# Storing a step's 32 output rows as one transfer of four quarters, or as four transfers of 32 partitions

## The chip, the core and the metric

The kernel runs on one core of a Trainium2 chip. The metric is device time in microseconds (us) for one execution; where several runs are given, their median counts. The core has five engines with instruction queues of their own: TensorE (PE), which multiplies matrices and loads weights for that beside it (PEld); VectorE (DVE); ScalarE (ACT); GpSimd (POOL); and SyncE (SP), which in this kernel only issues transfers. Transfers between main memory (HBM) and the core's on-chip memory of 128 partitions (SBUF) are moved by 16 DMA engines. An engine that issues a transfer goes on at once; when the bytes have landed, a semaphore is raised, and whoever needs them waits for it. Accumulators of matrix products lie in PSUM, from where ACT or DVE copy them out.

## The reference, cut to what matters

The output is two halves side by side. Part B (a long convolution of a state-space model) is finished before the part that this change touches. Part A is an attention with a recurrent memory: 64 segments of 32 tokens, one after the other, each with 8 memory rows that are the result of the segment before.

```python
for s in range(n_seg):                      # 64 segments of seg_len = 32
    xs = x[:, s * seg_len:(s + 1) * seg_len, :].copy()
    h = jnp.concatenate([mem, xs], axis=1)  # 8 memory rows + 32 tokens, Dm = 1024
    q = jnp.einsum('btd,dhe->bhte', h, Wq)  # 32 heads of 128
    k = jnp.einsum('btd,dhe->bhte', h, Wk)
    v = jnp.einsum('btd,dhe->bhte', h, Wv)
    scores = jnp.einsum('bhqe,bhke->bhqk', q, k) * scale
    scores = jnp.where(mask[None, None], scores, -1000000000.0)
    p = _softmax(scores, axis=-1)
    o = jnp.einsum('bhqk,bhke->bhqe', p, v)
    o = jnp.einsum('bhte,hed->btd', o, Wo)
    mem = o[:, :M, :].copy()                # M = 8
    outs.append(o[:, M:, :])
```

Everything is bf16. The weights Wq, Wk, Wv and Wo are 8 MB each; a segment needs all of them, and the next segment cannot start before the memory rows of this one are there.

## The kernel before, in words

Part A is `part_a` (L233). Its loop over `s` (L363) does one segment, called a step here, in about 20 us. 24 tokens' worth of every segment and the 8 memory rows go through the loop as one 32-column block `hT`; the other 8 tokens (their projections were made earlier) come in as small blocks from HBM and are finished after the loop (L592 to L623).

**Weights.** A weight block is 128 x 2048 bf16, 512 KB; a step uses 64 of them. 49 stay in SBUF, three are kept in PSUM and in odd places (`KEPT`, L29), and twelve are streamed again in every step from HBM into four slots `wst` that take turns (`SLOTS`, `stage`, L294 to L298). SP issues the twelve loads, each as soon as PE is done with the block that had the slot before. In the order of use, and by the names that the prediction gives them, they are

- L1: k, half 0, block 2; L2: q, half 0, block 2
- L3 and L4: k, half 1, blocks 1 and 5
- L5: q, half 1, block 4
- L6 and L7: v, half 0, blocks 2 and 7
- L8 and L9: v, half 1, blocks 4 and 7
- L10, L11, L12: output projection, blocks 4, 8 and 13

L1 to L4 of a step are issued during the step before.

**The order on PE** in a step (L484 to L580): the products k0, q0 and the first three blocks of k1 (`quads`, L364), the transposes of k0 and q0 (`tr`, L380), the rest of k1, the scores of the first half, q1, three blocks of v0, transposes of k1 and q1, the rest of v0, scores of the second half, v1, the products with the softmax weights, and the output projection (`oproj`, L474). Then the result is copied out into `ob`, its memory rows are transposed into `hT`, and the next step's k0 begins.

**The order on ACT**: copies of accumulators (`evac`, L375; its copy is L377), the exponentials, and four transfers in a step, which all stand in ACT's instruction queue. At the end of a step come the copies into `ob` (L574, L585, L588), `load_pk` for the next step (L333; called PK here), and `stores` (L348): first the store of the left-over block into `OLd` (L349; called OL), then the store of the 32 output rows (L353). Next on ACT's queue stand the copies of k0 and of q0 of the next step (both L377), the mask (L390), the copy of the transposed q0 (L497) and `load_vx` (L339; called VX).

**The rows in SBUF.** `ob[:, 0, :]` is 128 partitions x 256 elements: partitions 32q to 32q+31 hold the 32 rows of quarter q of the 1024 output columns (24 rows of tokens, and 8 memory rows whose places in the output are written again by L623 at the end). In HBM a row is 2048 elements wide (both parts), so each partition's 512 bytes go to a place of their own.

**What is written over `ob`.** `ob` lies in `arena`, a block whose regions are used again by hand (`AT`, L36). Its bytes are written next in the following step by the copy of q1 (`evac`, L377) and by the normalised weights (`weigh`, L423), which wait until the stores have landed.

**Completion semaphores.** The transfers of SP and ACT share eight completion semaphores (in the built program DMAHW0 to DMAHW7), handed out in turn when the program is built, over both queues together. A transfer waits, in its engine's queue, until the transfer that had its semaphore before has landed, which is the one eight places earlier in that turn. A step has 16 transfers, two whole turns: PK, OL, L5, the rows, L6, L7, VX, L8, L9, L10, L11, L12, and the next step's L1, L2, L3, L4.

Of the kernel before, what the change touches and what calls it, by code (L numbers as in the profile page):

```python
# [232 lines left out]
def part_a(ctx, tc, x, src, WD, HE, seg_len, out_a, ahead, W_res, rest, places, first):  # L233
    nc = tc.nc
# [47 lines left out]
    def at(name, *dims):  # L282

        n = int(np.prod(dims))
        t_ = arena[:, AT[name] // 2:AT[name] // 2 + n]
        if len(dims) == 1:
            return t_
        names = "abc"[:len(dims)]
        return t_.rearrange("p (%s) -> p %s" % (" ".join(names), " ".join(names)), **dict(zip(names, dims)))
# [58 lines left out]
    def stores(s, ob):  # L348
        nc.scalar.dma_start(out=OLd[s // 8][:, 256 * (s % 8):256 * (s % 8) + 256], in_=ob[:, 1, :])  # L349
        rows = out_a[s * SL:s * SL + SL, :].rearrange("r (q d) -> q r d", q=4)  # L350
        if s + 1 < NS:

            nc.scalar.dma_start(out=rows, in_=ob[:, 0, :])  # L353
        else:
            for q in range(4):
                nc.scalar.dma_start(out=rows[q][0:XM], in_=ob[32 * q:32 * q + XM, 0, :])
# [6 lines left out]
    for s in range(NS):  # L363
# [207 lines left out]
        ob = at("ob", 2, 256)  # L571
# [17 lines left out]
        if s + 1 < NS:  # L589
            stores(s, ob)  # L590
# [3 lines left out]
    for u in order:  # L594
        if ("o", u) in W_res:
            wo[u] = W_res["o", u]
        else:
# [3 lines left out]
            else:  # L601
                nc.sync.dma_start(out=wo[u][:].rearrange("e (h d) -> e h d", h=2), in_=src(("o", u)))
    stores(NS - 1, ob)
    for j in range(2, 8):
        nc.sync.dma_start(out=raw[j][:], in_=OLd[j])
# [926 lines left out]
```

## Time and profile before

| | |
|---|---|
| median of 3 runs | 2060.81 us (2054.64 to 2061.03) |
| profiled execution: its time, its span | 2054.64 us, 2054.6 us |
| PE busy in the span | 1873.8 us (91%) |
| ACT busy | 1051.7 us (51%) |
| stretch 760 to 1975 us (61 steps): PE busy, DMA share | 1162.56 of 1215 us, 0.95 |
| the same: bytes moved | 339 GB/s |
| last stage after the loop (L617) | about 55 us |

The steps run from about 720 us to 1994 us. In a profile, a line such as "L377 ACT CAST arena<-acc" is one group of instructions by source line, engine, operation and the names of what is written and read. "ACTq" and "SPq" are the instructions on ACT's and SP's queues that issue transfers. "idle before, releaser" is how long an engine sat before such instructions, and whose end let it go on.

### The profile page before, as it was taken

The page shows a single profiled execution, that of the slowest core. Times are in us where ns is not written, and L with a number is a line of the kernel's source. Part 1 is how long each engine was busy: PE and PEld are TensorE (multiplying, and loading weights), DVE is VectorE, ACT ScalarE, POOL GpSimd, SP SyncE. Part 2 cuts the span into 40 slices and gives each one's busy share as a digit, 9 for nine tenths or more (in the row PEclk, how much of TensorE's full clock was granted, in tenths as well). Part 3 has the DMA queues.
Part 4 walks back from the last instruction along what each step waited for, and adds up shares of the span by engine and source line. Part 5 has one row for each costly group of instructions (what it writes and reads, how often), then busy time and mean ns, then how long its engine had stood idle before and what let it go on. Part 6 is the DMA issues. An engine that isn't in the chain of part 4 may idle for free. (4 is left out here: it accounts for less than half of the span.)

```text
span 2054.6 us, 78607 instructions
## 1 busy us (share of the span) xinstructions
PE 1873.8 (91%) x33734; PEld 1187.8 (58%) x33734; DVE 1413.7 (69%) x3352; ACT 1051.7 (51%) x1981; POOL 398.5 (19%) x778
## 2 busy tenths in 40 slices
PE   2699999977999879999999999999999999999999
PEld 1365666666888535555555555555555555555554
DVE  8689989989999436666566666666666666656650
ACT  5899999961333324444344444444444444444430
POOL 2133343356000001111111111111111111111120
PEclk9999999989999989999999999999999999999999
DMA  7697986676646999999999999999999999999991
GB/s 192 176 247 217 262 227 181 164 207 204 217 140 190 330 328 350 349 337 335 315 347 342 343 339 342 343 342 339 347 345 333 339 332 341 335 333 339 342 356 46
DMA packets 349617, 590.25 MB, mean 287 GB/s; under 512 B 108536, under 2 KB 226520, under 8 KB 347220
## 3 DMA queue, kind: packets, MB, share of 16 engines
q1 hardware_dynamic: 294488, 526.49, 75.5%
q0 software_dynamic: 9968, 30.48, 4.5%
q10 hardware_dynamic: 44812, 28.26, 4.4%
q8 instruction: 264, 4.33, 0.9%
q14 instruction: 85, 0.70, 0.1%
HBM read 530.34 MB, written 65.26 MB: 290 GB/s over the span
## 5 line engine op out<-in xcount | busy, mean ns | idle before, releaser
L371 PEld LDWEIGHTS <-a_hT 128*32 128x32 bf16 x12352 | 334.4, 96 | 306.5 <-issue 59.4
L377 ACT CAST arena<-acc 128x512 bf16<-128x512 f32 x384 | 225.1, 586 | 375.6 <-PE acc L371 318.8
L371 PE MATMUL acc<-W,a_hT 128*32 128x512 bf16 x4608 | 371.7, 381 | 1.4 <-issue 1.2
L481 PEld LDWEIGHTS <-arena 128*32 128x32 bf16 x8256 | 212.1, 97 | 98.3 <-issue 47.1
L371 PE MATMUL acc<-wst,a_hT 128*32 128x512 bf16 x2304 | 231.9, 381 | 21.0 <-DMA wst<-WD_v 12.4
L292 DVE TENSOR_SCALAR arena<-keep 128x256 int32<-128x256 int32 (+1 forms) x512 | 176.3, 395 | 43.3 <-PE acc L371 39.8
L385 POOL COPY arena<-arena 128x128 bf16<-128x128 bf16 x128 | 37.5, 293 | 855.0 <-DMA arena<-PKd 312.3
L371 PE MATMUL acc<-MF,a_hT 128*32 128x512 bf16 x2048 | 171.3, 382 | 0.0
L481 PE MATMUL pp<-W_o,arena 128*32 128x256 bf16 x4096 | 138.4, 275 | 5.9 <-DMA W_o<-in_A_Wo_dram 5.8
L420 DVE TENSOR_REDUCE a_mx<-sc 128x4 f32<-128x160 f32 (+1 forms) x192 | 73.0, 380 | 81.8 <-ACT sc L416 81.8
L167 PE MATMUL pro<-xTl,wsl 128*128 128x512 bf16 x512 | 119.3, 384 | 9.6 <-ACT xTl L111 5.5
L412 DVE TENSOR_REDUCE a_mx<-sc 128x4 f32<-128x160 f32 (+1 forms) x192 | 72.0, 375 | 79.7 <-PE sc L400 78.2
L416 ACT ACTIVATE sc<-sc 128x160 f32<-128x160 f32 (+1 forms) x192 | 63.9, 333 | 120.9 <-DVE sc L413 101.8
L1066 PEld LDWEIGHTS <-MF 128*128 128x128 bf16 x1024 | 103.0, 101 | 29.9 <-issue 8.5
L443 POOL TENSOR_TENSOR arena<-arena,a_BD 128x128 bf16<-128x128 bf16 x128 | 71.2, 557 | 239.1 <-DVE arena L430 216.1
L496 DVE COPY arena<-tr 128x512 bf16<-128x512 bf16 x64 | 27.2, 425 | 128.3 <-PE tr L382 128.3
L1066 PE MATMUL hps<-KT,MF 128*128 128x256 bf16 x720 | 94.8, 285 | 14.0 <-DVE x L1235 11.0
L467 ACT CAST arena<-pv 128x256 bf16<-128x256 f32 (+1 forms) x192 | 79.0, 449 | 53.3 <-PE pp L450 41.0
L1293 PE MATMUL yp<-Bt,MI 128*128 128x256 bf16 x680 | 102.8, 273 | 0.8 <-ACT yb L1309 0.8
L574 ACT CAST arena<-pp 128x128 bf16<-128x128 f32 x128 | 27.7, 269 | 142.4 <-PE pp L481 142.4
L1104 ACT ACTIVATE E<-pa 128x648 bf16<-128x648 f32 x128 | 91.4, 714 | 17.6 <-PE pa L1096 12.1
L371 PE MATMUL acc<-W_v,a_hT 128*32 128x512 bf16 x1280 | 93.0, 380 | 0.5 <-issue 0.5
(314 smaller groups left out, 3988.2 us busy)
## 6 DMA issues: line engine op xcount, KB each, us to landing
wst<-WD_v SPq DMA_DIRECT2D x256, 512.0 KB
wst<-WD_k SPq DMA_DIRECT2D x192, 512.0 KB
wst<-WD_o SPq DMA_DIRECT2D x192, 512.0 KB
wst<-WD_q SPq DMA_DIRECT2D x128, 512.0 KB
Ud<-ux POOLq DMA_DIRECT2D x16, 1024.0 KB, 5.1
uq<-Ud SPq DMA_DIRECT2D x32, 512.0 KB
wsl<-in_A_Wk_dram SPq DMA_DIRECT2D x16, 512.0 KB
wsl<-in_A_Wv_dram SPq DMA_DIRECT2D x16, 512.0 KB
```

Of the source, the lines that this page charges most:

```text
L167: nc.tensor.matmul(a[:], lhsT=w[:, kc, 128 * j:128 * j + 128], rhs=xTl[:, kc, :, :].rearrange("p s k -> p (s k)"), start=(kc == 0), stop=( ...
L292: nc.vector.tensor_scalar(out=out.bitcast(I32), in0=in_.bitcast(I32), scalar1=0, scalar2=None, op0=ALU.bitwise_or)
L371: nc.tensor.matmul(a[32 * g:32 * g + 32, o_:o_ + rhs.shape[1]], lhsT=hT[:, kc, :], rhs=rhs, start=(kc == 0), stop=(kc == KC - 1), tile_pos ...
L377: nc.scalar.copy(out=q, in_=a[:])
L412: nc.vector.tensor_reduce(out=m_, in_=x, axis=AX.X, op=ALU.max)
L420: nc.vector.tensor_reduce(out=m_, in_=x, axis=AX.X, op=ALU.add)
L443: nc.gpsimd.tensor_tensor(out=L[:, 0].rearrange("p (a b) k -> p a b k", a=4), in0=bc(lt[:, :, 0:XL].unsqueeze(2), [128, 4, 4, XL]), in1=bc ...
L467: nc.scalar.copy(out=o[:, i:i + n], in_=p[:, i:i + n, :].rearrange("p a (g q) -> p a g q", g=4))
L481: nc.tensor.matmul(po[32 * qt:32 * qt + 32, o_:o_ + rhs.shape[1]], lhsT=oT[:, h % 4, (h % 16) // 4, :], rhs=rhs, start=False, stop=(h == 3 ...
L1066: pe.matmul(s_[r][half][:, cs, :], lhsT=MF[:, kc, 4 * rr + mc, cs, :], rhs=rhs, start=(i == 0 and mc == 0), stop=(i == 1 and mc == 3), ski ...
L1104: sc.activation(out=T["E", r, e // 4][:, lo:lo + 8 * NE].rearrange("p (i c) -> p i c", i=2), in_=T.pop(("p", r, e))[:, :, 0:4 * NE], func= ...
L1293: pe.matmul(yp[:, b, :], lhsT=m_[:, b, cs, kc, :], rhs=Bt[:, kc, j, half, c_, :], start=(kc == 0 and cs == 0 and half == 0), stop=(kc == 3 ...
```

## The change

In `stores`, the transfer of the output rows, for every step but the last, becomes a loop of four transfers, one for each quarter of the columns. They are issued by the same engine at the same place in its queue, and move the same bytes in the same 512-byte pieces. The last step already had such a loop over 24 of the 32 partitions of each quarter (L356), which stays.

```diff
         rows = out_a[s * SL:s * SL + SL, :].rearrange("r (q d) -> q r d", q=4)
         if s + 1 < NS:
 
-            nc.scalar.dma_start(out=rows, in_=ob[:, 0, :])
+            for q in range(4):
+                nc.scalar.dma_start(out=rows[q], in_=ob[32 * q:32 * q + 32, 0, :])
         else:
             for q in range(4):
                 nc.scalar.dma_start(out=rows[q][0:XM], in_=ob[32 * q:32 * q + XM, 0, :])
```

The order of all other instructions on every engine stays as it was. The number of transfers of SP and ACT in a step goes from 16 to 19, and the eight completion semaphores are handed out over these.

## The prediction

> **What bounds the kernel now.** I read the page first, then the stretch of the steps, then PE's waits in it. The change acts 63 times, once at each boundary between two steps, so the stretch from 760 to 1975 us (61 steps) is what counts. Columns: stretch, its length, busy time of PE, PEld, DVE, ACT and POOL, TensorE clock, DMA share, GB/s.
>
> ```profile
> 760.00:1975.00 1215.00, 1162.56 (x26046) 682.78 (x26041) 763.13 (x2391) 548.79 (x1287) 176.98 (x429) 1.00 0.95 339
> ```
>
> PE is busy 1162.56 of 1215 us at full clock, and the DMA engines carry 339 GB/s without a pause. Who made PE wait there (us in total, times, longest):
>
> ```profile
> PE acc L371 <- DMA wst<-WD_v: 9.1, 16, 1.2
> PE pp L481 <- DMA wst<-WD_o: 7.3, 13, 1.1
> PE acc L371 <- DMA wst<-WD_k: 4.8, 9, 1.5
> PE tr L382 <- ACT arena L377: 2.3, 3, 1.4
> PE acc L371 <- DMA wst<-WD_q: 1.4, 4, 0.5
> ```
>
> Weights cost PE only 22.6 us in 61 steps (0.37 us a step): PE is the bound, but the stream runs just ahead of it. From the landing events of the loads, step by step, a load lands at a median of 0.26 to 0.78 us before PE uses it. That is all the slack there is.
>
> Now one boundary, ACT and then SP in order of time:
>
> ```profile
> 1754.46 0.33 ACTq L333 DMA_DIRECT2D arena<-PKd  x1
> ...
> 1755.20 0.33 ACTq L349 DMA_DIRECT2D OLd<-arena  x1
> 1755.57 0.57 ACTq L353 DMA_DIRECT2D out_dram<-arena  x1
> 1757.29 0.59 ACT L377 CAST arena<-acc 128x512 bf16<-128x512 f32 x1 [2.12 <-PE acc L371]
> 1758.95 0.59 ACT L377 CAST arena<-acc 128x512 bf16<-128x512 f32 x1 [1.08 <-PE acc L371]
> 1759.57 0.43 ACT L390 CAST sc<-a_mask 128x320 f32<-128x320 bf16 x1
> ```
>
> ```profile
> 1752.67 2.60 SPq L297 DMA_DIRECT2D wst<-WD_k  x2
> 1755.87 0.32 SPq L297 DMA_DIRECT2D wst<-WD_q  x1
> 1757.81 5.51 SPq L297 DMA_DIRECT2D wst<-WD_v  x4
> ```
>
> ACT issues the rows at 1755.57 and has 1.15 us to spare before k0's copy. SP issues L3 and L4, then L5, then L6 at 1757.81. In the chain of work the pieces named DMA run from issue to landing:
>
> ```profile
> 1736.81 7.50 DMA out_dram<-arena
> ...
> 1755.87 6.65 DMA wst<-WD_q
> ...
> 1769.04 7.16 DMA wst<-WD_k
> ```
>
> A transfer takes 5 to 7 us, because some four loads are queued. From the landing events, with time zero at the issue of OL, medians of 39 steps: L1 lands at -0.27, L2 at 1.44, L3 at 3.24 (one in ten after 4.27), L4 at 5.13, PK at 5.18, OL at 5.58, L5 at 6.80, the rows at 6.71, L6 (issued at 2.62) at 8.30, L7 (issued at 4.13) at 10.01, L8 (issued at 5.68) at 11.57.
>
> **The change, part by part.** The sum is made against the profiled execution (2054.6 us, whose own time 2054.64 is the lowest of the three); it is then put on the median, 2060.81.
>
> *Three more issues on ACT, 63 times.* The rows of L353 and L356:
>
> ```profile
> L353 ACTq DMA_DIRECT2D out_dram<-arena x63: 552/562/1144, 741.9 to 1974.0; - x63
> L356 ACTq DMA_DIRECT2D out_dram<-arena x4: 308/444/675, 1995.4 to 1997.7; - x4
>   ACT arena L377: 6.8, 6
>   DVE arena L423: 3.3, 4
> ```
>
> One issue of 562 ns becomes four of 308 to 444 ns: 1.23 to 1.78 us, that is 0.7 to 1.2 us more. k0's copy follows 1.15 us after the old issue, so by itself this is hidden.
>
> *The turn of the eight semaphores.* This I take to be the main effect. With 19 transfers in a step the turn is PK, OL, L5, R0, R1, R2, R3, L6, L7, VX, L8 to L12, L1 to L4 (R0 to R3 are the four pieces), and each waits for the one eight places earlier. In the listing of the built kernel R0 waits for L12, R1 for L1, R2 for L2, R3 for L3; L6 for L4, L7 for PK, VX for OL, L8 for L5, and L9 to L12 for R0 to R3. Before, the rows waited for L12 and L6 for nothing later than L2.
> That ACT does stand still for such a wait shows in the last step, which has the split already:
>
> ```profile
> 1995.35 2.65 ACTq L356 DMA_DIRECT2D out_dram<-arena  x4
> ```
>
> Its four issues last 0.68, 0.51, 0.38 and 0.31 us, 1.88 together; of the 2.65, 0.70 us lie before the fourth, which goes 0.02 us after the load with its semaphore before it (an L600 load) has landed.
>
> (a) ACT. R3 cannot be issued before L3 has landed, at 3.24, and ends at 3.57. Behind it on ACT stand k0's copy (2.09 before, then 3.6 to 4.2) and q0's (3.75 before, then 4.2 to 4.8); PE's transposes of q0 (L382) wait for that, then the copy of L497 and the scores. I moved the two copies in each of the 39 steps to where that step's landing of L3 lets them: q0's copy comes 0.37 us later in the mean (median 0.22, one in ten over 0.84). PE has nothing else to do there, so 0.37 us a step is on the path.
>
> (b) SP. L6 goes at 5.18 instead of 2.62 (2.33 us late in the mean), L7 at 5.5 instead of 4.13, L8 at 6.85 instead of 5.68. When L6 is issued, only L5 and small pieces are still queued, so it should travel faster than its 5.56 us. Four 512 KB loads that met an empty queue in part B (uq, L1040) landed 3.69 to 4.01 us after issue. So L6 lands at 8.9 to 9.2. PE wants it at 8.30 + 0.37 slack + 0.37 from (a) = 9.04: between nothing and 0.16 us; L7 and L8, each some 1.55 us behind L6, likewise. The nearest row of the other kind is that a load keeps its 5.56 us: 10.74, 1.70 us a step late. I take 0.2, near the first end, because the queue ahead of it is almost empty, with something added for steps that scatter.
>
> (c) VX waits for OL: 5.58 instead of its 4.90. ACT's next work is k1's copy at about 6.4: hidden. L9 to L12 wait for pieces that land before 8 and are issued after that anyway or nearly so: nothing.
>
> *The bytes over the engines.* The queue of ACT moved these packets (count, MB, share of the 16 engines' span):
>
> ```profile
> q10 hardware_dynamic: 44812, 28.26, 4.4%
> ```
>
> Its data are 40,928 packets (PK and VX 8,192 each, OL 8,192, the stores of part B 8,192, the rows 8,064, the last 96); the other 3,884 are one closing packet for each engine that took part. 224 transfers on 16 engines and 4 on 12 make 3,632; that leaves 252 for the 63 stores, 4 each. So the store runs on four engines, 32 packets on each, and after the change on all 16, two of each piece. A 512-byte packet takes 27 ns in the trace: 0.86 us on each of four engines becomes 0.22. By the Trainium skill, "DMA: Bandwidth & Descriptors", section "Why a DMA increments its semaphore by 16 and not by 1", the number of engines is the largest up to 16 that divides the slowest dimension of both sides, 4 for four quarters and 16 for 32 partitions. The trace's 252 agrees with that. What can come of it: the loads' wait, at most the 22.6 us above, and the stores' wait (6.8 and 3.3 us in the rows of L377 and L423). Between 0 and 0.5 us a step; I take nothing, since the slack was there and (b) drains the queue.
> The same page's "Rules for kernel authors" says not to split a transfer into disjoint partition ranges, as they share the same engines; by that rule alone the gain would be nil. Here four engines became 16, which is another case.
>
> Sum: 0.37 + 0.2 = 0.57 us a step, times 63 = 36 us. 2054.6 becomes 2090.6, and the median 2060.8 becomes 2097.
>
> **The rivals.**
> *The queue runs dry.* If late loads keep their 5.56 us, (b) is 1.70 instead of 0.2: 2.07 x 63 = 130 us, 2191. For it: 5 to 7 us in every chain piece. Against it: the 3.69 to 4.01 us of loads that met an empty queue.
> *Even engines, faster.* If the four busy engines are what makes loads land late, all of PE's waits for weights and stores go: 22.6 + 10.1 = 33 us at most, 2028, and the turn's waits must be hidden. It decides if (a) and (b) together stay under 0.5 us a step. Against it: the sixteen landings of a load are spread evenly over about 2 us, without four that stand apart. Half of it would be 2044.
> *Nothing.* L3 lands early enough and L6's slack holds, or gain and loss cancel: within 0.3% (about what a measurement of this kernel can tell from no change: the three runs spread by 0.31%), 2061.
>
> **How the numbers follow.** Forecast (12 to 85 us more, by (a) alone from its median to (b) at half its upper end): 0.69. Queue runs dry: 0.10. Faster: 0.12. Nothing: 0.09. A range over the forecast alone is 2073 to 2146; with half of the faster case the low end is 2044, and the dry queue's upper half is left out. Slower 0.79, within 0.3% 0.09, faster 0.12.
>
> **What would show it.** L354 four times a boundary, with a gap of 1 to 2 us before the fourth; k0's copy no longer released by PE but behind ACT's own queue; more waits of PE's L382 on ACT L377 (2.3 us now, some 20 expected); L6 issued about 2.5 us later and landing after 4 to 5 us; the waits for the stores gone from L377 and L423; 3,780 more closing packets on ACT's queue. I am wrong if PE's waits for weights fall, or if the gap before the fourth piece is missing.

## The result, and the profile after

The kernel with the four pieces takes 2128.13 us (median of 4 runs, 2119.72 to 2135.83), against 2057.95 us (4 runs, 2054.64 to 2061.03) for the kernel before beside it. The ratio is 1.0342, with a 95% interval from 1.0305 to 1.0380: some 70 us, or 1.1 us for each of the 63 boundaries. The forecast was 36 us more (2097), with a range up to 2146. The sign and the range held; the size was half of what came.

In the changed kernel everything behind L353 is one line lower: PE's L371 is L372, L382 is L383, L481 is L482; ACT's L377 is L378; DVE's L423 is L424. The profiled execution took 2122.51 us, span 2120.8 us.

The view by stretches, with the same columns as before. The first line is the whole stretch of the steps (about 61, as in the 1215 us shown of before). The others are single microseconds of one boundary, whose OL is issued at 1767.09:

```profile
760.00:2040.00 1280.00, 1173.81 (x26070) 685.92 (x26066) 768.64 (x2396) 545.90 (x1287) 176.51 (x429) 1.00 0.91 322
...
1770.09:1771.09 1.00, 1.00 (x27) 0.59 (x20) 0.42 (x2) 0.18 (x1) 0.00 (x0) 1.00 1.11 367
1771.09:1772.09 1.00, 1.00 (x22) 0.39 (x15) 0.00 (x0) 0.99 (x2) 0.00 (x0) 1.00 0.99 384
1772.09:1773.09 1.00, 1.00 (x20) 0.67 (x22) 0.42 (x1) 0.88 (x2) 0.29 (x1) 1.00 0.36 120
1773.09:1774.09 1.00, 0.66 (x40) 0.32 (x28) 0.00 (x0) 0.13 (x1) 0.00 (x0) 1.00 0.81 236
1774.09:1775.09 1.00, 0.98 (x24) 0.54 (x28) 0.63 (x2) 0.46 (x1) 0.00 (x0) 1.00 0.99 395
```

Read the last two columns, the share of the DMA engines and GB/s. Over the stretch they fell from 0.95 and 339 to 0.91 and 322; the clock is 1.00 in both. At this boundary the DMA engines drop to 0.36 and 120 GB/s in the sixth microsecond after OL, and in the next one PE is busy for only 0.66 us. PE's gap there is not a wait for a load: the view of waits gives 0.4 us of it to L401, with no releaser. Averaged over 60 steps, the sixth and seventh microseconds after OL carry 148 and 222 GB/s, against 360 and 346 in the kernel before. The same two microseconds of the boundary shown of before (OL at 1755.20) have no such hole:

```profile
1760.20:1761.20 1.00, 1.00 (x52) 0.65 (x48) 0.09 (x1) 0.47 (x1) 0.26 (x1) 1.00 1.01 384
1761.20:1762.20 1.00, 1.00 (x28) 0.51 (x19) 0.73 (x2) 0.59 (x1) 0.00 (x0) 1.00 1.14 386
```

Who made PE wait, in the kernel after (us in total, times, longest):

```profile
PE acc L372 <- DMA wst<-WD_v: 57.3, 71, 2.5
PE pp L482 <- DMA wst<-WD_o: 7.1, 12, 1.8
PE acc L372 <- DMA wst<-WD_k: 5.1, 10, 1.3
PE acc L372 <- DMA wst<-WD_q: 3.9, 7, 0.9
PE tr L383 <- ACT arena L378: 3.5, 11, 0.4
```

The wait for v blocks went from 9.1 to 57.3 us; the four lines of weights together went from 22.6 to 73.4. Sorted by load (PE's idle time before the first product of each in these stretches, worked out from the trace), L6 cost 20.3 us (2.9 before), L7 19.9 (0.9) and L8 14.4 (4.4): 46 us more on these three, 5 us more on the nine others.

The last line of that view is the one that the forecast put most on: PE waiting for ACT's copies. It went from 2.3 to 3.5 us only. But a transpose reads the copied block as its weights, so most of this wait stands in the rows of the weight loads (PEld), first before, then after:

```profile
PEld L382 <- ACT arena L377: 7.7, 18, 1.6
PEld L383 <- ACT arena L378: 32.6, 81, 0.9
```

The transposes of k0 and q0 have 29.6 of the 32.6 us (3.0 before). What PE itself loses by it shows in the stretch from its first use of L3 to its first use of L4, which holds these transposes. In the mean of 60 steps it went from 1.56 to 1.79 us, 0.23 us more. The three stretches that end with the first use of L6, L7 and L8 grew by 0.36, 0.32 and 0.18 us, 0.86 together. The whole step grew by 1.06.

The stretch of the steps is 65 us longer: 54 us of it is idle time of PE, 11 us is busy time. L372's rose from 717.91 to 732.53 us and L383's from 76.38 to 80.61, L482's fell from 257.14 to 253.12, for nearly the same number of products. Ends of products are modelled in the profile. The busy time grew most in the same four stretches (by 0.25 us a step together), so it is probably waiting that counts as work; that isn't shown.

Now the same boundary of the kernel after on ACT and on SP, in order of time:

```profile
1767.09 0.33 ACTq L349 DMA_DIRECT2D OLd<-arena  x1
1767.46 3.41 ACTq L354 DMA_DIRECT2D out_dram<-arena  x4
1770.91 1.17 ACT L378 CAST arena<-acc 128x512 bf16<-128x512 f32 x2 [3.85 <-DMA OLd<-arena]
...
1772.68 0.34 ACTq L339 DMA_DIRECT2D arena<-VXd  x1
```

```profile
1764.64 1.63 SPq L297 DMA_DIRECT2D wst<-WD_k  x2
1768.42 0.32 SPq L297 DMA_DIRECT2D wst<-WD_q  x1
1772.22 3.75 SPq L297 DMA_DIRECT2D wst<-WD_v  x4
```

The four pieces hold ACT's queue for 3.41 us (0.57 before), and k0's and q0's copies (the pair at 1770.91) come right behind. Of the 3.41 us, the issues themselves are 1.50; the rest is waiting, 0.99 us of it ahead of the last piece, which goes 0.02 us after L3 has landed at 1770.53. On SP, L6 goes at 1772.22, 0.07 us after L4 has landed at 1772.15; that is 5.13 us after OL, where it was 2.61 at the boundary shown of before. From the issue of L5 at 1768.42 to 1772.22 SP hands out nothing, and that is the hole seen above. At this one boundary PE doesn't pay for it: L7 and L8 still land 0.41 and 0.04 us before their first products. The price is in the other steps, where PE waits for v blocks 71 times.

### The profile page after: what moved, and what is told of

Its sections match the earlier page's. It is cut to its first block, busy times and chain, and to the rows that moved or that the text cites. A ratio compares the mean times of both kernels' runs of the same rounds, so it can differ in the third digit from the quotient of the medians.

```text
span 2120.8 us, 78957 instructions
## 1 busy us (share of the span) xinstructions
PE 1884.1 (89%) x33706; PEld 1190.5 (56%) x33734; DVE 1418.4 (67%) x3352; ACT 1048.5 (49%) x1981; POOL 398.3 (19%) x778
## 5 line engine op out<-in xcount | busy, mean ns | idle before, releaser
L372 PEld LDWEIGHTS <-a_hT 128*32 128x32 bf16 x12352 | 333.7, 96 | 381.5 <-issue 131.8
L378 ACT CAST arena<-acc 128x512 bf16<-128x512 f32 x384 | 221.2, 587 | 419.8 <-PE acc L372 158.7
L372 PE MATMUL acc<-W,a_hT 128*32 128x512 bf16 x4608 | 372.4, 383 | 0.3 <-issue 0.2
L372 PE MATMUL acc<-wst,a_hT 128*32 128x512 bf16 x2304 | 232.1, 384 | 72.2 <-DMA wst<-WD_v 61.3
L482 PEld LDWEIGHTS <-arena 128*32 128x32 bf16 x8256 | 214.4, 97 | 90.1 <-issue 45.2
L386 POOL COPY arena<-arena 128x128 bf16<-128x128 bf16 x128 | 37.4, 292 | 901.8 <-PE tr L383 309.9
L372 PE MATMUL acc<-MF,a_hT 128*32 128x512 bf16 x2048 | 171.2, 382 | 0.3 <-PE acc L372 0.3
L482 PE MATMUL pp<-W_o,arena 128*32 128x256 bf16 x4096 | 138.2, 275 | 5.7 <-DMA W_o<-in_A_Wo_dram 5.6
L444 POOL TENSOR_TENSOR arena<-arena,a_BD 128x128 bf16<-128x128 bf16 x128 | 64.5, 504 | 216.2 <-DVE arena L431 175.7
L439 DVE TENSOR_TENSOR arena<-arena,a_BDL 128x384 bf16<-128x384 bf16 (+1 forms) x128 | 86.9, 679 | 26.1 <-POOL arena L386 22.4
```

The lines of the kernel that those rows point to most:

```text
L372: nc.tensor.matmul(a[32 * g:32 * g + 32, o_:o_ + rhs.shape[1]], lhsT=hT[:, kc, :], rhs=rhs, start=(kc == 0), stop=(kc == KC - 1), tile_pos ...
L378: nc.scalar.copy(out=q, in_=a[:])
L439: eng.tensor_tensor(out=out, in0=bc(pl.unsqueeze(1), [128, m, n]), in1=bc(BDL[:].rearrange("p a b -> p (a b)")[:, j:j + m].unsqueeze(2), [ ...
L482: nc.tensor.matmul(po[32 * qt:32 * qt + 32, o_:o_ + rhs.shape[1]], lhsT=oT[:, h % 4, (h % 16) // 4, :], rhs=rhs, start=False, stop=(h == 3 ...
```

## The experiments

Times of the kernel before in these runs: 2055.62 to 2058.34 us, each time measured beside the experiment. Where the text gives times "after OL", they are medians over the steps from the landing events, as in the prediction.

**More transfers without the split.** The store of the rows stays whole, on four engines; three small transfers of 16 partitions are added behind it, so that the turn of the semaphores has 19 places as in the change.

```diff
             nc.scalar.dma_start(out=rows, in_=ob[:, 0, :])
+            nc.scalar.dma_start(out=ahead.SCRd[s, 0:16, 0:128], in_=ident[0:16, :])
+            nc.scalar.dma_start(out=ahead.SCRd[s, 16:32, 0:128], in_=ident[0:16, :])
+            nc.scalar.dma_start(out=ahead.SCRd[s, 32:48, 0:128], in_=ident[0:16, :])
```

> The store of the rows stays one transfer on four DMA engines; behind it ACT issues three tiny transfers (16 partitions of a constant, 256 bytes each, to a scratch buffer). A step has 19 transfers, and the semaphores' turn gives the same waits as the changed kernel: the third tiny one waits for L3, L6 for L4, L7 for PK, L8 for L5. Theory 1 (the turn's waits cost the time): as slow as the changed kernel, 2110 to 2140 us, PE's waits for WD_v about 50 us. Theory 2 (the splitting of the store itself, with pieces that land later, costs it): 2055 to 2075 us, since the store is whole here.

Measured: 2121.79 us (2114.82 to 2124.38), ratio 1.0305 (1.0280 to 1.0330). Most of the 3.4% is there without any split. L6 is issued 5.03 us after OL and lands at 9.08 (5.05 and 8.90 in the change).

**The same three on SP's queue**, between L5 and L6: the same turn, but ACT doesn't stand still.

```diff
         pt0 = turn(weigh(sc0, None, "pn0"), "pt0")
+        if s:
+            nc.sync.dma_start(out=ahead.SCRd[s, 0:16, 0:128], in_=ident[0:16, :])
+            nc.sync.dma_start(out=ahead.SCRd[s, 16:32, 0:128], in_=ident[0:16, :])
+            nc.sync.dma_start(out=ahead.SCRd[s, 32:48, 0:128], in_=ident[0:16, :])
```

> As the run with three tiny transfers on ACT, but SP issues them, between L5 and L6; the turn is the same, and ACT's queue never stands still for L3. Theory 1a (the late loads L6 to L8 are most of the price): 2100 to 2130 us, with ACT's copy of k0 back at 2.1 us after OL. Theory 1b (ACT standing still is most of it): 2060 to 2080 us.

Measured: 2113.97 us (2108.35 to 2137.72), ratio 1.0294 (1.0231 to 1.0358). k0's copy is at 2.09 us after OL and q0's at 3.75, as in the kernel before (3.47 and 3.98 in the change), and the loss is the same within the intervals:

```profile
PE acc L372 <- DMA wst<-WD_v: 62.6, 82, 3.1
```

This is PE's wait for v blocks there (760 to 2030 us); the change has 57.3. PE's stretch with the transposes is 1.58 us here (1.56 before), and 1.81 with the three transfers on ACT. So the late loads are enough for nearly the whole loss. What ACT's standing still adds isn't settled: 8 us by the two medians, between nothing and 20 by the ends of the two intervals.

**One and two more transfers.** The first line, or the first two, of the added three.

> One tiny transfer behind the whole store on ACT: 17 transfers in the turn. L6 waits for L2 (lands at 1.35 us after OL), L7 for L3 (3.2, wants to go at 4.1), L8 for PK (5.2, wants to go at 5.7): none of it late. Theory 1 (the turn): 2053 to 2064 us. Theory 3 (each transfer more has a price of its own, a third of the 63 us of three): about 2079 us.

> Two tiny transfers: 18 in the turn. L6 waits for L3 (3.2 instead of 2.6 us), L7 for L4 (5.0 instead of 4.1), L8 for OL (5.6, as it wants to go). The loads are late by less than a load's 1.55 us, so the DMA engines should not run dry. Theory 1: 2055 to 2075 us, and no slice of a step with much less than 300 GB/s. Theory 3: about 2100 us.

Measured: one more, 2059.18 us, ratio 1.0007 (0.9983 to 1.0032), nothing; two more, 2091.66 us, ratio 1.0163 (1.0139 to 1.0186), more than was expected. With one more, every load goes at the time that it had. With two, L6 goes only 0.38 us later (3.00) and still lands at 8.47 (8.30 before), but L7 goes at 5.03 instead of 4.13. PE's idle time by load is 23.3 us on L7 there, against 0.9 before, and 3.7 on L6 (2.9 before). The expectation that the DMA engines would not run dry held. In the mean of 60 steps no microsecond between 5 and 11 us after OL carries less than 292 GB/s (346 before). The time lay over its range all the same.

The loss goes with the bytes that aren't moved. Between 5 and 11 us after OL the queues of SP and ACT move 2108 KB in the kernel before, in the mean of 60 steps; with two more it is 1893 and in the change 1666. The missing 215 and 442 KB are 0.63 and 1.30 us of the stream at its 339 GB/s. The steps grew by 0.58 (19.83 to 20.41) and 1.06 us (to 20.89). With three more on ACT and on SP, 1.24 and 1.14 us are missing, and the steps grew by 1.09 and 0.87. A likely reason is that the DMA engines were busy for 0.95 of the time before, so what is left out at a boundary is hardly made up later; of the 1.30, some 0.24 was. The match alone doesn't prove it: a step that takes longer for any reason moves fewer bytes in a fixed stretch, since its loads are the same. For the three runs with 19 transfers the order in time speaks for it: the hole lies 5 to 7 us after OL, and PE begins to wait for L6 at 8.6 to 8.8.

**The store on 16 engines, as one transfer.** It goes to a scratch block in HBM with the partitions outermost, so the rows of the output are not written.

```diff
-            nc.scalar.dma_start(out=rows, in_=ob[:, 0, :])
+            nc.scalar.dma_start(out=ahead.SCRd[s], in_=ob[:, 0, :])
```

> One transfer of the rows per step, but to a scratch buffer of 128 contiguous rows of 512 bytes, so that it runs on 16 engines; the output's rows are left unwritten for 63 steps. The turn of the semaphores is that of the kernel before. If the spread over 16 engines is worth something: 2030 to 2050 us, with PE's waits for weights below 20 us in the steps. If it is hidden: 2053 to 2062 us.

Measured: 2054.46 us, ratio 0.9982 (0.9964 to 1.0000). ACT's queue has 45,568 packets there, 756 more than before, which is 12 more closing packets for each of the 63 stores: 16 engines instead of four. Four busy engines instead of sixteen cost at most 0.36%; between that and nothing this can't say.

**The four pieces on GpSimd's queue**, whose transfers have completion semaphores of their own:

```diff
-            nc.scalar.dma_start(out=rows, in_=ob[:, 0, :])
+            for q in range(4):
+                nc.gpsimd.dma_start(out=rows[q], in_=ob[32 * q:32 * q + 32, 0, :])
```

> The four pieces of 32 partitions, issued by GpSimd at the same place in the program instead of ACT. GpSimd's transfers have semaphores of their own, so a step has 15 transfers in the turn, and L6 waits for L12 only. Theory 1: no slower than before, 2040 to 2065 us. Theory 2 (splitting costs): 2110 us or more.

Measured: 2059.78 us, ratio 1.0015 (1.0001 to 1.0030). The pieces of 32 partitions cost next to nothing by themselves, if they have no part in the shared turn: L6 goes at 2.62 and lands at 8.34.

**Two transfers of 64 partitions**, on ACT:

```diff
-            nc.scalar.dma_start(out=rows, in_=ob[:, 0, :])
+            for q in range(2):
+                nc.scalar.dma_start(out=rows[2 * q:2 * q + 2], in_=ob[64 * q:64 * q + 64, 0, :])
```

> The store as two transfers of two quarters (64 partitions) each: 17 in the turn, as with one tiny transfer, and each on two DMA engines, 64 packets on each if both take the same two. Theory 1 alone: as the run with one tiny transfer, 2053 to 2064 us. If it matters on how few engines the store lies: 10 us or more above that run, and the rows land later than 6.7 us after OL.

Measured: 2184.00 us (2182.25 to 2190.09), ratio 1.0625 (1.0602 to 1.0649): the largest loss of all. The turn has 17 places, as with one more small transfer, which cost nothing; L6, L7 and L8 go and land as before. What is late is the store. Its first half lands 6.49 us after OL, but its second at 10.05 (the whole store: 6.71). The copy of q1, which is written over `ob`, goes from 8.32 to 10.24, and PE's transposes wait for it. The step grew by 2.03 us, and PE's stretch from L6 to L7, which holds these transposes, by 2.07. Not all of that is waiting: the granted clock in the steps (760 to 2100 us) was 0.96, where it was 1.00 before, and PE's busy time in them rose from 1162.56 to 1196.29 us. The view of PE's waits, and the packets on ACT's queue, of this kernel:

```profile
PE tr L383 <- ACT arena L378: 105.6, 43, 5.4
```

```profile
q10 hardware_dynamic: 44812, 28.26, 4.2%
```

44,812 packets are as many as before: 252 closing packets, now for 126 transfers, so each half uses two engines. The Trainium skill, "DMA: Bandwidth & Descriptors", section "Why a DMA increments its semaphore by 16 and not by 1", says the same for a slowest dimension of two, and that they are the lowest-numbered ones, so both halves would use the same two. The late second half agrees with that, but no run here separates "two engines" from "the same two". The Trainium skill, "DMA: Bandwidth & Descriptors", section "Rules for kernel authors", says of two transfers of disjoint halves that each uses all 16 engines; by the count of packets that isn't so here.

**The four pieces on ACT with the turn put right.** PK, OL and VX are issued by GpSimd, so that SP and ACT have 16 transfers in a step again. In a second version VX stands behind GpSimd's copy of the transposed keys (`put_kl`, L386 there) instead of ahead of it. The first version, on top of the change, and then what the second adds to it:

```diff
-        nc.scalar.dma_start(out=pk, in_=PKd[j])
+        nc.gpsimd.dma_start(out=pk, in_=PKd[j])
-        nc.scalar.dma_start(out=vx[:, 0:n], in_=VXd[j + 1, :, 0:n])
+        nc.gpsimd.dma_start(out=vx[:, 0:n], in_=VXd[j + 1, :, 0:n])
-        nc.scalar.dma_start(out=OLd[s // 8][:, 256 * (s % 8):256 * (s % 8) + 256], in_=ob[:, 1, :])
+        nc.gpsimd.dma_start(out=OLd[s // 8][:, 256 * (s % 8):256 * (s % 8) + 256], in_=ob[:, 1, :])
```

```diff
-        vx = load_vx(s)
         quads("k", 1, range(3, 7), a)
...
         put_kl(KT0, 0)
+        vx = load_vx(s)
         scores(0, sc0, QT0, KT0)
```

> The four pieces stay on ACT, and the other three transfers of ACT (PK, OL, VX) are issued by GpSimd: the turn has 16 transfers again, L6 waits for L2, L7 for L3, L8 for L4, and the last two pieces for L12 and L1. Theory 1: the price is gone, 2045 to 2070 us. Theory 2 (the four pieces on ACT's queue cost by themselves): 2100 us or more.

> As four_act (four pieces on ACT; PK, OL and VX issued by GpSimd, so that the shared turn is 16 again), but VX is issued behind GpSimd's copy L386 instead of ahead of it. If the some 30 us that four_act still lost came from that copy standing behind VX's issue (0.54 us on GpSimd's queue, 29.4 us of PE's waits of L397 for L386), those waits go and the time is 2050 to 2066 us. If they came from the four pieces on ACT or from the transfers of 32 partitions themselves, the time stays at 2080 to 2092 us.

Measured: 2086.25 us, ratio 1.0144 (1.0116 to 1.0172), and with VX moved 2061.91 us, ratio 1.0022 (0.9999 to 1.0045). The first lies in the range of neither theory. In it, the waits for v blocks were gone, but a new one stood in their place. PE's waits and GpSimd's order of time in the first version:

```profile
PE sc L397 <- POOL arena L386: 28.9, 56, 0.6
```

```profile
1743.63 0.54 POOL L339 DMA_DIRECT2D arena<-VXd  x1 [4.60 <-ACT arena L498]
1744.39 0.29 POOL L386 COPY arena<-arena 128x128 bf16<-128x128 bf16 x1 [0.23 <-DMA arena<-PKd]
```

An issue on GpSimd takes 0.54 us and stood right before a copy that PE's scores wait for. With VX behind that copy the wait is 0.5 us, and some 24 us are back: what the first version lost was mostly the order on this one queue.

**Only PK and OL on GpSimd**: with the four pieces (on top of the change), and as a control with the one store (on top of the kernel before). The edit is the same in both:

```diff
-        nc.scalar.dma_start(out=pk, in_=PKd[j])
+        nc.gpsimd.dma_start(out=pk, in_=PKd[j])
-        nc.scalar.dma_start(out=OLd[s // 8][:, 256 * (s % 8):256 * (s % 8) + 256], in_=ob[:, 1, :])
+        nc.gpsimd.dma_start(out=OLd[s // 8][:, 256 * (s % 8):256 * (s % 8) + 256], in_=ob[:, 1, :])
```

> Four pieces on ACT, PK and OL issued by GpSimd, VX by ACT as before: 17 transfers share the turn. By the built kernel's listing L6 waits for L2, L7 for L3, L8 for the first piece and VX for L4, so no weight load is held longer than before, and the last piece waits for L1 alone. If the whole loss of the change is the turn, the time is 2050 to 2066 us and L6 goes 2.6 us after OL and lands at 8.3 to 8.5. If four issues on ACT cost by themselves, k0's copy comes later than 2.1 us and the time is 2080 us or more.

> The kernel before, its one store of the rows kept, with PK and OL issued by GpSimd and nothing else changed. It tells what moving these two does by itself. If the four pieces are free once the turn is right, as the run with the four pieces and the same move says (2055.47 us against 2057.05), this lies within 0.3% of the kernel before and within 0.3% of that run: 2050 to 2064 us. If the move gains by itself and hides a price of the pieces, this is 2050 us or less, some 0.5% under the kernel before.

Measured: four pieces 2055.47 us, ratio 1.0000 (0.9983 to 1.0016); one store 2054.40 us, ratio 0.9990 (0.9961 to 1.0019). The four pieces stand on ACT's queue as in the change, and the loss is gone. A boundary of the kernel with the four pieces, on ACT and on SP:

```profile
1750.55 0.33 ACTq L354 DMA_DIRECT2D out_dram<-arena  x1
1750.56 0.30 ACT L589 CAST arena<-pl 128x128 bf16<-128x128 f32 x1
1750.92 1.59 ACTq L354 DMA_DIRECT2D out_dram<-arena  x3
1752.98 0.59 ACT L378 CAST arena<-acc 128x512 bf16<-128x512 f32 x1 [2.12 <-PE acc L372]
```

```profile
1751.57 0.32 SPq L297 DMA_DIRECT2D wst<-WD_q  x1
1753.51 6.44 SPq L297 DMA_DIRECT2D wst<-WD_v  x4
```

The pieces end at 1752.51, before k0's copy, which is again released by PE after the same 2.12 us; L6 goes 0.53 us after that copy begins (0.52 at the boundary shown of before). None of these versions is faster than the kernel before by more than the measurement can tell.

## Why the prediction was right, and where its sum was not

*Three more issues on ACT, hidden:* right. With the turn put right (PK and OL on GpSimd) they end 0.47 us before k0's copy at the boundary shown, and the time is unchanged. Of the 3.41 us that they take in the change itself, 1.91 is waiting for their semaphores.

*The turn of the eight semaphores as the main effect:* right, and shown from both sides. The turn of 19 without a split costs 3.05% or 2.94%; the split with a turn of 17 in which no weight load is held up costs nothing (1.0000, control 0.9990). With 17 and one small transfer it costs nothing either.

*(a) ACT stands still, 0.37 us a step on the path:* the event was right, and the price is not settled. q0's copy came 0.23 us later in the median (0.22 forecast). It reaches PE: its wait for the copies stands in the rows of the weight loads (32.6 us, 7.7 before; "some 20" more was expected, on PE's own row), and PE's stretch with the transposes grew by 0.23 us a step, and by 0.02 where the three transfers are on SP. But with ACT kept free nearly the same loss stayed (2.94% against 3.05%). Between nothing and 20 us, at most 0.3 us a step, are due to it.

*(b) SP, 0.2 us a step:* this is the term that was much too small. L6 went at 5.05 and landed at 8.90 after OL, inside the forecast 8.9 to 9.2; that part was right, and its 3.91 us of travel came near the loads that had met an empty queue. But with L6 landing on time for its own use "and L7 and L8 likewise", I had priced a late issue only by that one load's landing. L7 landed 2.2 us behind L6 and L8 2.0 us behind L7 instead of "some 1.55" (1.71 and 1.56 by the prediction's own landings), at 11.13 and 13.13, that is 1.15 and 1.53 us later than before. And even on L6 the wait was 17 us more in 61 steps, 0.28 us: PE was ready for it at 8.84 in the median (9.04 forecast), and half of the landings come later than their median. The term was 0.76 us a step by PE's waits on L6 to L8, and 0.86 by the growth of the three stretches that end with them.

What this term left out, as far as the runs show it: an almost empty queue, which I counted as a gain for L6's travel, is also bytes not moved. In the sixth microsecond after OL the stream carries 148 GB/s instead of 360, and a stream that was busy for 0.95 of the time has little room to make that up. So the rival "the queue runs dry" was half right: the queue did run dry, and L7 and L8 took 5.6 and 6.1 us, but L6, on which that rival was priced, travelled in 3.91 and did not keep its 5.56. The 70 us lie a third of the way from the forecast's 36 to that rival's 130. That sign and range held while a term was 0.2 instead of 0.8 is owed in part to the width of the range.

*(c) VX hidden; L9 to L12 nothing:* VX came at 5.59 at the boundary shown, as forecast (5.58). L9 to L12 are issued later, but so is the step; the waits on the nine other loads grew by 5 us in all.

*Spread over 16 engines, taken as nothing:* right within what can be told. The packets on ACT's queue went up by exactly 3,780:

```profile
q10 hardware_dynamic: 48592, 28.28, 4.5%
```

The rival "even engines" had a ceiling of 33 us; the store on 16 engines alone brought 0.18% (3.9 us by the medians), with an interval that reaches to no gain at all.

*What would show it:* four issues of L354 at each boundary, but the standing still was spread over them (issued 0.37, 1.03, 1.98 and 3.06 us after OL in the median) and not all before the fourth. k0's copy is no longer released by PE: the view of ACT's waits puts it down to a DMA 53 times (the groups of `OLd`, `wst` and `out_dram`), which are only the last events ahead of it; the 36.9 us that it now gives for waits on the rows are of this kind, about 4 us each, the length of k0's idle time. On L424 the wait for the store went from 3.3 to 0.4 us, as forecast. PE's waits for weights didn't fall, and at the boundary shown the gap before the fourth piece was 0.99 us.

## What to carry to other kernels

Where transfers of several queues share a few completion semaphores in turn, count the transfers of one loop pass before adding any, and list for each load which transfer it then has to wait for: one more was free here, two cost 1.6%, three 3%, though the bytes of one such transfer cost nothing that could be measured. A load that is issued late can still land on time and the stream lose, so price the gap in the queue in bytes too, at the rate of the stream, and not only by the landing of the first late load; here that came within 0.3 us of a step's growth in four runs. If a split is wanted, move other small transfers off the shared turn first, and look at what stands behind them on the queue that they move to.

## What was not expected of the hardware

- One added transfer of 16 partitions x 128 elements cost nothing that could be measured (1.0007), yet two of them cost 1.63% and three 3.05%, through the waits for shared semaphores.
- Two stores of 64 partitions on two engines each landed at 6.49 and 10.05 us after OL, where one store on four engines landed at 6.71. The run with them took 6.25% longer, at a granted clock of 0.96 in the steps, while going from four engines to sixteen brought at most 0.36%.
- After the hole, L7 and L8 travelled for 5.6 and 6.1 us although the queue had been nearly empty just before (5.7 and 5.8 in the kernel before). Which of the transfers then under way (L6, VX, the pieces' last ones) held them isn't settled.
